# Two more tiles take their second product by seven products, and attention runs ahead of the tiles through DRAM

## The chip, the cores and the metric

The kernel runs on one core of one Trainium2 chip. Its time is the device time of one execution in microseconds (us); a comparison uses the median of the runs. The engines are named as in the profile: PE is TensorE's matrix multiplication and PEld its weight loads, DVE is VectorE, ACT is ScalarE, POOL is GpSimd, SP is SyncE, which here issues every DMA.

## The reference

The program is a linear attention with an RMS norm, followed by a feed-forward block with a SiLU gate. Everything is float32.

```python
q, k, v: (8 batches, 8 heads, 576 tokens, 64)     g_norm: (64,)
kv  = einsum('bhsd,bhse->bhde', k, v)             # 64 x 64 per batch and head
o   = einsum('bhsd,bhde->bhse', q, kv)
o   = o / sqrt(mean(o*o, -1) + 1e-6) * g_norm
x   = o.transpose(0, 2, 1, 3).reshape(4608, 512)  # tokens x features
h   = x @ w_in                                    # 512 -> 2048: the first product
out = (h * sigmoid(h)) @ w_out                    # 2048 -> 512: the second product
```

## The kernel before, in words

**Precision.** Every float32 operand of a product is held as two parts, an upper one rounded to the multiplier's format and a lower one, the rest. A product is three matmuls: upper by lower, lower by upper, upper by upper. The names ending in h and l (gh and gl, qh and ql) are such pairs.

**Tiles, blocks and steps.** The 4608 tokens are cut into nine tiles of 512, numbered 0 to 8. The hidden features are 16 blocks of 128, and the whole program is counted in blocks: block g = 16 t + n is place n of tile t, so tile 2 begins at block 32, tile 5 at block 80 and tile 7 at block 112. A batch of attention has 576 tokens, so it straddles two tiles.

**How a tile is multiplied.** Tiles 0 and 1 do both products plainly. From tile 2 on, the first product goes by seven products in place of eight (Strassen's scheme in Winograd's form, on halves of the weights and of x): two blocks are one step, and a step has 7 x 6 = 42 matmuls of 256 columns for it (`product`, L709), on sums of weight blocks that were formed once in tile 1, put into DRAM (`make_sums`) and loaded anew for each step (`load_sums`, L638). In `pair_step` (tiles 2 to 6) the second product is plain: 2 blocks x 4 banks x 3 terms x 2 halves = 48 matmuls per step (`project`, L494). In `seven_step` (tiles 7 and 8) the second product goes by seven products too: 42 matmuls per step (`multiply`, L880), with forms of the gated activations that DVE builds and sums of the second weights which `make_out_sums` has put into DRAM before and `load_out_sums` (L961) loads into small buffers for each step.

**Around a pair step.** PE does products 1, 2, 6 and 7; ACT copies product 1 (L761), DVE adds products 2, 6 and 7 to it (L762 to L764); PE does products 4, 5 and 3 into the same banks, and DVE adds those (L774 to L779). Then PE does the 48 matmuls of the step before. Product 5 writes the bank half that L762 has read.

**Around a seven step.** The products alternate in one bank with windows of the second product's matmuls. DVE reads the bank with L1075, L1093, L1107, L1108 and, behind product 3, L1116; the next step's product 1 waits for L1116. At the last three steps of tile 7, `spread_switch` and `made_ahead` form the operands of tile 8 in spare buffers, because tile 7's are in use to the end; `after_switch` empties the banks of tile 7 during the first steps of tile 8.

**Attention.** `plan(b, g)` books the work of batch b from block g on: k and v are loaded in blocks g-7 to g-4, their product (`kv_block`, L274) comes in block g-2, q is loaded from g-1 on, each of the four head pairs c is split in block g+c (L294, L295, L288), multiplied in g+2+c (`mm_out`, L307 to L309), squared and summed in g+3+c (L319, L320); the norms follow in blocks g+7 and g+8, and from g+9+c on `spread` (L327) lays out the norm and `scale` (L335) writes the scaled output. It writes straight to where a tile's x lies in full precision, two buffers called x32. A batch begins every 16 blocks, `plan(b, (b - 1) * NF)`, and its second part, which belongs to the next tile, is scaled in that tile.

**Order.** The order on each engine is the order in which the code is written (a manual schedule). Lists of jobs by block (`first_jobs`, `mid_jobs`, `last_jobs`) are run at the start, middle and end of a block. Each engine works its own queue in that order, SP's DMA issues too. Buffers turn in rings: the eight `kvq` buffers hold k, v, q and its parts (and in seven steps the gated activations and loaded sums), five `tmp` buffers hold passing work, four `opool` buffers hold attention's unscaled output o.

## Time and profile before

| | |
|---|---|
| median of 3 runs | 812.39 us (811.72 to 812.76) |
| the profiled execution | 813.5 us, span of its instructions 811.7 us |
| PE, PEld busy | 800.1 us (99%), 794.5 us (98%) |
| DVE, ACT, POOL busy | 585.2, 391.2, 194.5 us |
| granted TensorE clock | 0.998 |
| matmul records | 7388 |
| moved by DMA | 145.90 MB, 51.3% of the DMA engines' time in the kernel's own queue |

A row of groups reads: line, engine, operation, tile written <- tiles read (buffer numbers left out), shape, count | busy us, mean ns of one | idle time of the engine just before. A row of the timeline begins with the start from the span's beginning, and the time that it covers; [0.37 <-DVE gated L1116] is idle time before it and what ended it. A row of windows gives, for a stretch of time, the busy time and the count of PE, PEld, DVE, ACT and POOL, then the granted clock, the DMA engines' busy share and GB/s. The busy time of a matmul (277 ns) is longer than the distance from one to the next (113 ns), since they are pipelined: counts and starts tell the pace, busy time does not.

The tiles stand in the trace at these times: tile 2 from 203.2 us, and one more every 87.6 us up to tile 6 from 553.5 us; tile 7 from 641.1 us and tile 8 from about 724 us.

### The profile page before, as it was taken

To read this page: it belongs to the slowest core of one execution; us is meant where nothing else is said; L and a number is where in the kernel's file an instruction comes from. 1 tells how busy PE (TensorE), PEld (TensorE's weight loads), DVE (VectorE), ACT (ScalarE), POOL (GpSimd) and SP (SyncE) were. 2 spreads that over 40 slices of the span, in tenths; PEclk is the share of its full clock that TensorE was granted. 3 is DMA by queue.
4 is the path that set the end of the run, shared out by engine and by line. 5 is a ranking of instruction groups with operands and counts; after the bars stand their busy time and mean duration, and the time that the engine had idled before them with its cause. 6 is when DMAs were issued, how large, how long until landed. Compare 5 with 4: busy or idle time off the path is not lost.

```text
span 811.7 us, 18340 instructions
## 1 busy us (share of the span) xinstructions
PE 800.1 (99%) x7388; PEld 794.5 (98%) x7388; DVE 585.2 (72%) x1184; ACT 391.2 (48%) x825; POOL 194.5 (24%) x191
## 2 busy tenths in 40 slices
PE   8999999999999999999999999999999999999997
PEld 7899999999999999999999999999999999999996
DVE  4999956787566667757876667667875777788666
ACT  4887555434552255425642455336532543455443
POOL 2799783332110014020332014201402000000000
PEclk9999999999999999999999999999999999999999
DMA  9994012356434444465545462555443576667553
GB/s 350 412 409 127 1 60 78 131 182 248 167 101 162 163 155 140 142 218 190 170 152 179 154 236 91 204 185 193 147 140 104 187 253 212 214 209 223 198 185 115
DMA packets 60248, 145.90 MB, mean 180 GB/s; under 512 B 5891, under 2 KB 21251, under 8 KB 60163
## 3 DMA queue, kind: packets, MB, share of 16 engines
q1 hardware_dynamic: 60162, 144.73, 51.3%
q8 instruction: 58, 0.95, 0.5%
q14 instruction: 28, 0.22, 0.1%
HBM read 118.49 MB, written 26.21 MB: 178 GB/s over the span
## 4 chain that ended last, share of the span: by engine, by line
PE 91%; DMA 4%; POOL 2%; DVE 1%; issue 1%; ACT 0%; SPq 0%; DVEq 0%; POOLq 0%; ACTq 0%
PE acc L494 36%; PE hp L709 33%; PE hp L494 9%; PE acc L880 5%; DMA wi<-in_moe_w_in 3%; PE at L880 3%; PE at L274 2%; PE hp L880 1%; DMA k<-in_k 1%; PE at L307 1%; PE at L308 1%; PE at L309 1%; POOL wo L213 1%; DMA early_wo<-in_q 1%; POOL wi L213 0%
## 5 line engine op out<-in xcount | busy, mean ns | idle before, releaser
L494 PE MATMUL acc<-wo,gh 128*128 128x256 f32 x1792 | 279.6, 277 | 0.1
L494 PEld LDWEIGHTS acc<-wo,gh 128*128 128x128 f32 x1792 | 238.6, 188 | 0.6 <-POOL wo L213 0.3
L494 PE MATMUL acc<-wo,gl 128*128 128x256 f32 x896 | 174.5, 276 | 0.0
L709 PE MATMUL hp<-x_second,wi 128*128 128x256 f32 x1248 | 156.9, 277 | 0.0
L709 PEld LDWEIGHTS hp<-x_second,wi 128*128 128x128 f32 x1248 | 148.8, 188 | 0.0
L494 PEld LDWEIGHTS acc<-wo,gl 128*128 128x128 f32 x896 | 134.8, 188 | 0.0
L709 PE MATMUL hp<-operand,wi 128*128 128x256 f32 x1008 | 126.6, 277 | 0.4 <-DVE gated L1116 0.4
L709 PEld LDWEIGHTS hp<-operand,wi 128*128 128x128 f32 x1008 | 120.1, 188 | 0.6 <-DVE gated L1116 0.6
L295 POOL TENSOR_TENSOR ql<-q,qh 128x576 fp32r<-128x576 f32 x24 | 34.8, 1449 | 261.0 <-ACT qh L294 225.2
L761 ACT COPY wi<-hp 128x256 f32<-128x256 f32 x40 | 14.9, 372 | 92.6 <-PE hp L709 92.6
L719 ACT ACTIVATE gh<-gf 128x512 fp32r<-128x512 f32 x40 | 25.3, 633 | 57.1 <-DVE gf L774 52.5
L931 POOL TENSOR_TENSOR e<-e,partial 128x256 f32<-128x256 f32 x2 | 1.5, 730 | 190.3 <-DVE e L931 190.3
L494 PE MATMUL hp<-x_second,wi 128*128 128x256 f32 x384 | 46.3, 277 | 0.0
L826 ACT ACTIVATE gated<-gated 128x512 f32<-128x512 f32 x32 | 20.3, 633 | 52.8 <-DVE gated L1107 39.8
L494 PE MATMUL hp<-x,wi 128*128 128x256 f32 x360 | 44.5, 278 | 0.8 <-POOL x L445 0.8
L494 PEld LDWEIGHTS hp<-x_second,wi 128*128 128x128 f32 x384 | 44.9, 188 | 0.1
L603 POOL TENSOR_TENSOR s<-wo 128x512 f32<-128x512 f32 x16 | 21.6, 1353 | 93.3 <-DVE x L335 40.8
L494 PEld LDWEIGHTS hp<-x,wi 128*128 128x128 f32 x360 | 42.4, 188 | 1.1 <-POOL x L445 1.0
L719 ACT ACTIVATE gh<-wi 128x512 fp32r<-128x512 f32 x40 | 25.4, 635 | 36.8 <-DVE wi L774 32.8
L335 DVE SCALAR_TENSOR_TENSOR x<-o,gcol,yT 128x128 f32<-128x128 f32 (+7 forms) x52 | 41.2, 792 | 1.9
L762 DVE TENSOR_TENSOR wi<-hp,wi 128x256 f32<-128x256 f32 x20 | 8.5, 424 | 45.7 <-ACT wi L761 45.7
L313 ACT ACTIVATE sq<-at 128x256 f32<-128x256 f32 (+1 forms) x56 | 22.9, 409 | 37.8 <-PE at L309 37.5
(213 smaller groups left out, 1465.6 us busy)
## 6 DMA issues: line engine op xcount, KB each, us to landing
wi<-sums_in_dram SPq DMA_DIRECT2D x112, 512.0 KB, 3.3
s<-out_sums SPq DMA_DIRECT2D x48, 256.0 KB, 4.5
wi<-in_moe_w_in SPq DMA_DIRECT2D x16, 512.0 KB, 8.1
wo<-in_moe_w_out SPq DMA_DIRECT2D x16, 512.0 KB, 9.1
sums_in_dram<-sum_parts SPq DMA_DIRECT2D x16, 512.0 KB, 2.6
out_sums<-wi SPq DMA_DIRECT2D x16, 512.0 KB, 2.7
k<-in_k SPq DMA_DIRECT2D x28, 288.0 KB, 4.7
v<-in_v SPq DMA_DIRECT2D x28, 288.0 KB, 5.2
```

The lines of the kernel that those rows point to most:

```text
L274: nc.tensor.matmul(out=self.kv[h], lhsT=self.k[rows, c, :], rhs=self.v[rows, c, :], start=(start and r == 0), stop=(stop and r == 4),)
L295: (nc.vector if self.b == 1 else nc.gpsimd).tensor_tensor(out=self.ql, in0=self.q, in1=self.qh.bitcast(F32), op=ALU.subtract)
L313: nc.scalar.activation(out=self.sq[:, self.w], in_=self.ps, func=AF.Square)
L335: nc.vector.scalar_tensor_tensor(out=to, in0=self.o[:, a:e], scalar=gcol, in1=self.yT, op0=ALU.mult, op1=ALU.mult)
L494: nc.tensor.matmul(out=to[:, at:at + 256], lhsT=stationary, rhs=moving[:, at:at + 256], start=start and at == 0, stop=stop and at == n - 256,)
L603: nc.gpsimd.tensor_tensor(out=to, in0=w[:, 0, :], in1=w[:, 1, :], op=ALU.add)
L709: nc.tensor.matmul(out=out, lhsT=a_of(i, a, c), rhs=x[b][:, c], start=start and n == 0, stop=n == 5, skip_group_check=not check,)
L719: nc.scalar.activation(out=gh, in_=x, func=AF.Silu)
L761: nc.scalar.copy(out=p1, in_=u)
L762: nc.vector.tensor_tensor(out=c1[:, low], in0=v, in1=p1, op=ALU.add)
L826: nc.scalar.activation(out=self.gated, in_=self.gated, func=AF.Silu)
L880: nc.tensor.matmul(out=self.out[m], lhsT=g[m], rhs=self.weight(m, j, a), start=j == 0 and n == 0 and m in self.opens, stop=j == HF - 1 and ...
```

## The change

- `OUT7` goes from 7 to 5: tiles 5, 6, 7 and 8 run as seven steps, tiles 2 to 4 as pair steps.
- The batches of attention begin at blocks 16, 26, 36, 45, 55 and 64 (batches 2 to 7) in place of 16, 32, 48, 64, 80 and 96. Loads of k and v come one block later relative to that.
- From batch 3 on, `spread` and `scale` work on all 576 tokens of a head pair in one piece and write back to o in place. `keep`, one block later, stores o to a new DRAM tensor `x_in_dram` by tile, and `load_x` brings a tile's x back into the x32 buffers during the tile before (batch 2 does the same with its part that belongs to tile 3).
- The eight `make_out_sums` begin at blocks 34, 37, 40, 50, 53, 56, 66 and 69 in place of 52, 60, ... 108.
- `spread_switch` runs in tiles 5, 6 and 7. The spare buffers for the first two operands are taken once; later switches use the buffers that the switch before has freed.

```diff
-    OUT7 = 7
+    OUT7 = 5
+    AT = {1: 3, 2: 16, 3: 26, 4: 36, 5: 45, 6: 55, 7: 64}
...
+    x_in_dram = dram.tile([NT, 2, P, 2, TN], F32, name="x_in_dram")
+
+    def load_x(t):
+        for row in range(2):
+            nc.sync.dma_start(
+                out=late(row, [P, 2, TN], F32, f"x32_{row}").rearrange("p c n -> p (c n)"),
+                in_=x_in_dram[t, row].rearrange("p c n -> p (c n)"),
+            )
...
         def spread(self, y, segment):
-            a, e, _, _ = segments(self.b)[segment]
+            a, e = (0, S) if segment is None else segments(self.b)[segment][:2]
...
         def scale(self, segment):
-            a, e, t, o = segments(self.b)[segment]
-            to = self.o[:, a:e] if t < 2 else x32(self.c, slice(o, o + e - a))
+            a, e, t, o = (0, S, 3, 0) if segment is None else segments(self.b)[segment]
+            to = x32(self.c, slice(o, o + e - a)) if t == 2 else self.o[:, a:e]
...
+        def keep(self):
+            for a, e, t, o in segments(self.b):
+                if t > 2:
+                    nc.sync.dma_start(out=x_in_dram[t, self.c // 2][:, self.c % 2, o:o + e - a], in_=self.o[:, a:e])
...
     def spread_switch():
...
-        ahead.update({
-            1: spares, 6: [block6[:, 0], block6[:, 1]], 2: home(1), 7: home(6), 4: home(2), 5: home(7), 3: home(4),
-        })
+            once["spares"] = spare1, [block6[:, 0], block6[:, 1]]
+        ahead.update(zip((1, 6), once["spares"]))
+        ahead.update({2: home(1), 7: home(6), 4: home(2), 5: home(7), 3: home(4)})
+        once["spares"] = home(5), home(3)
...
-            for p, i in zip(ps, (-7, -6, -5, -4)):
-                at(first_jobs, g + i, lambda p=p: p.load(which="kv"))
+            for p, jobs, i in zip(ps, (last_jobs, first_jobs, first_jobs, first_jobs), (-6, -5, -4, -3)):
+                at(jobs, g + i, lambda p=p: p.load(which="kv"))
...
+        def x_stages(p, s, *parts):
+            for part in parts:
+                at(mid_jobs, s, lambda part=part: p.spread(norms[1][:, p.c], part), lambda part=part: p.scale(part))
+            if b > 1:
+                at(first_jobs, s + 1, p.keep)
...
-                x_stages(p, s + 2 + p.c, 0)
-            x_stages(p, b * NF + (1, 4, 6, 8)[p.c] if b >= OUT7 else b * NF + 1 + p.c, 1)
+                x_stages(p, s + 2 + p.c, *((0, 1) if b == 2 else (None,)))
...
-            plan(b, (b - 1) * NF)
+            plan(b, AT[b])
...
-        for j in range(HF):
-            spread_out(lambda j=j: make_out_sums(j), 3 * (3 * NF + 4 + 8 * j), 1, 1, 1, 1, 1, 1, 1, 1)
+        for t in range(3, NT):
+            at(last_jobs, max((t - 1) * NF + (5 if t - 1 > OUT7 else 2), AT.get(t, 0) + 14), lambda t=t: load_x(t))
+        for j, g in enumerate((34, 37, 40, 50, 53, 56, 66, 69)):
+            spread_out(lambda j=j: make_out_sums(j), 3 * g, 1, 1, 1, 1, 1, 1, 1, 1)
```

The lines of the changed file stand 10 to 18 places further down than those of the kernel before: L327 (spread) is L337 there, L335 (scale) L345, L701 (lower parts of the operands) L716, L723 (gl) L738, L762 to L764 are L777 to L779, L774 to L779 are L789 to L794, L839, L842, L847 are L854, L857, L862, and L1116 is L1134.

DVE in the first step of the first tile that runs as seven steps; before, this is tile 7 (block 112). The names are those of the forms (wi_8882) and of the half's gated activations; yT and o are attention's.

```order
L1107 TENSOR_TENSOR gated<-hp,wi_3139 128x256
L1108 TENSOR_TENSOR gated<-hp,wi_3139 128x256
L839 TENSOR_TENSOR wi_8882<-gated 128x256
L842 TENSOR_TENSOR wi_8882<-gated,wi_8882 128x128
L327 STREAM_TRANSPOSE yT<-y 128x512
L335 SCALAR_TENSOR_TENSOR x_0_1952<-o,gcol,yT 128x512
L1116 TENSOR_TENSOR gated<-hp,wi_3139 128x256
L847 TENSOR_TENSOR wi_8882<-gated,wi_8882 128x128
```

The same place in the changed kernel, tile 5 (block 80):

```order
L1125 TENSOR_TENSOR gated<-hp,wi_3269 128x256
L1126 TENSOR_TENSOR gated<-hp,wi_3269 128x256
L854 TENSOR_TENSOR wi_7035<-gated 128x256
L857 TENSOR_TENSOR wi_7035<-gated,wi_7035 128x128
L1134 TENSOR_TENSOR gated<-hp,wi_3269 128x256
L862 TENSOR_TENSOR wi_7035<-gated,wi_7035 128x128
```

Attention's spread and scale of the last batch no longer stand between the sums of the bank.

DVE in the last step of tile 2 (blocks 46 and 47), before:

```order
L723 TENSOR_TENSOR gl<-wi_3139,gh 128x512
L701 TENSOR_TENSOR operand_2948<-x_0_1952,operand_2948 128x512
L701 TENSOR_TENSOR operand_2952<-x_1_2124,operand_2952 128x512
L701 TENSOR_TENSOR operand_2987<-t_4031,operand_2987 128x512
L701 TENSOR_TENSOR x_second<-x_0_1952,x_second 128x512
L774 TENSOR_TENSOR wi_3139<-hp,wi_3139 128x512
L778 TENSOR_TENSOR gf<-hp,wi_3139 128x256
L779 TENSOR_TENSOR gf<-hp,gf 128x256
L701 TENSOR_TENSOR x_second<-t_4032,x_second 128x512
L701 TENSOR_TENSOR x_second<-t_4030,x_second 128x512
L701 TENSOR_TENSOR x_second<-x_1_2124,x_second 128x512
L723 TENSOR_TENSOR gl<-wi_3139,gh 128x512
```

and in the changed kernel, from the row of the fourth operand on (the rows ahead of it, gl and three operands, are as before):

```order
L716 TENSOR_TENSOR x_second<-x_0_1953,x_second 128x512
L337 STREAM_TRANSPOSE yT<-y 128x576
L345 SCALAR_TENSOR_TENSOR o<-o,gcol,yT 128x576
L789 TENSOR_TENSOR wi_3269<-hp,wi_3269 128x512
L793 TENSOR_TENSOR gf<-hp,wi_3269 128x256
L794 TENSOR_TENSOR gf<-hp,gf 128x256
L716 TENSOR_TENSOR x_second<-t_4337,x_second 128x512
L716 TENSOR_TENSOR x_second<-t_4335,x_second 128x512
L716 TENSOR_TENSOR x_second<-x_1_2125,x_second 128x512
L298 TENSOR_TENSOR kl<-kvm_91,kh 128x128
L738 TENSOR_TENSOR gl<-wi_3269,gh 128x512
L337 STREAM_TRANSPOSE yT<-y 128x576
```

A spread and a scale now stand ahead of L789 (before: L774), a second pair and two kl follow: attention's batch 4 is scaled and batch 5 split while the operands of tile 3 are made.

SP at the same turn in the changed kernel, last step of tile 2 and first of tile 3. The rows L653 load the sums of the first weights for the next step, L352 are the stores of `keep`:

```order
L352 DMA x_in_dram<-o 128x256
L352 DMA x_in_dram<-o 128x320
L273 DMA q<-in_q 128x576
L653 DMA wi_3083<-sums_in_dram 128x1024
L653 DMA wi_3085<-sums_in_dram 128x1024
L352 DMA x_in_dram<-o 128x256
L352 DMA x_in_dram<-o 128x320
L352 DMA x_in_dram<-o 128x256
L352 DMA x_in_dram<-o 128x320
L653 DMA wi_3083<-sums_in_dram 128x1024
```

Before, at this turn, nothing but loads of q and the stores of the tile's result stood between these loads at a turn of tiles. Now each pair of stores that waits for `scale` has loads of sums behind it.

More of the change, by code (lines that the diff above doesn't have):

```diff
@@ L985, in spread_switch @@
     def spread_switch():
[L987 to L994 removed]
+        if "spares" not in once:
+            once["partial"] = opool.tile([P, S], F32, name="partial", tag="o")[:, :TN].rearrange("p (j n) -> p j n", n=H)
+            spare1 = [
+                opool.tile([P, S], F32R, name="moved", tag="o")[:, :TN].rearrange("p (k n) -> p k n", k=2)
+                for _ in range(2)
+            ]
+            block6 = block("wi", HF + 7, F32R).rearrange("p a (k n) -> p a k n", k=2)
+            once["spares"] = spare1, [block6[:, 0], block6[:, 1]]
+        ahead.update(zip((1, 6), once["spares"]))
+        ahead.update({2: home(1), 7: home(6), 4: home(2), 5: home(7), 3: home(4)})
+        once["spares"] = home(5), home(3)
         x = sums_of_x()
@@ L1234, in linear_attention_rms_silu_ffn @@
         g_stats, stats = stats[:, 256:257], stats[:, :64].rearrange("p (c i j) -> p c i j", i=2, j=8)
-        second = plan(1, 3)
+        second = plan(1, AT[1])
         for item in ORDER.split():
```

10 lines of the change are left out of this document (1 added, 9 removed).

## The prediction

> **What bounds the kernel now.** I read the page's busy shares first, then the list of PE's waits, then the chain of waits through a pair step, and last the timeline of PE and DVE around the one wait that falls inside the tiles which change.
>
> ```profile
> PE 800.1 (99%) x7388; PEld 794.5 (98%) x7388; DVE 585.2 (72%) x1184; ACT 391.2 (48%) x825; POOL 194.5 (24%) x191
> PE 91%; DMA 4%; POOL 2%; DVE 1%; issue 1%; ACT 0%; SPq 0%; DVEq 0%; POOLq 0%; ACTq 0%
> PE hp L709 <- DVE gated L1116: 0.4, 1, 0.4
> ```
>
> PE is busy nearly to the end, 91% of the chain is PE, and the longest wait behind the start-up is 0.4 us, so the time is the number of matmuls times the distance from one to the next. That distance is read from the chain in tile 4:
>
> ```profile
> 360.76 4.76 PE hp L709 x42
> 365.52 5.44 PE acc L494 x48
> 370.96 4.76 PE hp L709 x42
> ```
>
> Starts follow each other without a hole: 42 matmuls of 256 columns in 4.76 us and 48 in 5.44 us are 113.3 ns each. A seven step has 84 of them, 9.52 us at this pace. But tile 7 does not keep it, and the windows of six steps of tile 7 and of five steps of tile 8 show this:
>
> ```profile
> 664.50:723.87 59.37, 59.37 (x507) 59.37 (x506) 46.28 (x107) 26.93 (x55) 0.00 (x0) 1.00 0.65 215
> 743.02:790.82 47.80, 47.80 (x422) 47.80 (x421) 31.04 (x79) 19.90 (x41) 0.00 (x0) 1.00 0.63 205
> ```
>
> 59.37 / 6 = 9.895 us a step in tile 7 (117.8 ns a matmul), 47.80 / 5 = 9.56 in tile 8. Granted clock (1.00 and 1.00) and DMA share (0.65 and 0.63) are alike, so neither is the reason. The timeline of PE shows where the slower pace begins and ends:
>
> ```profile
> 651.93 0.84 PE L709 MATMUL hp<-x_second,wi 128*128 128x256 f32 x6
> 654.51 1.68 PE L709 MATMUL hp<-operand,wi 128*128 128x256 f32 x12 [0.37 <-DVE gated L1116]
> 723.87 0.87 PE L709 MATMUL hp<-moved,wi 128*128 128x256 f32 x6
> 724.57 0.88 PE L709 MATMUL hp<-wi,wi 128*128 128x256 f32 x6
> 725.28 0.40 PE L880 MATMUL at<-wo,gh 128*128 128x256 f32 x2
> 743.02 0.84 PE L709 MATMUL hp<-moved,wi 128*128 128x256 f32 x6
> 743.70 0.87 PE L709 MATMUL hp<-wi,wi 128*128 128x256 f32 x6
> 744.41 0.40 PE L880 MATMUL at<-wo,gh 128*128 128x256 f32 x2
> ```
>
> Ahead of the wait six matmuls take 0.84 us (the last one's pipeline included), behind it six take 0.87: the pace turns from 113 to 118 ns at the 0.37 us wait and stays until 724.57, where product 6 of tile 8 reads its x from a weight block. From the first start behind the wait to the start of tile 8, 723.87 - 654.51 = 69.36 us pass for seven steps, against 7 x 9.52 = 66.6. The same thing happens once in the start-up, and there with other work:
>
> ```profile
> 24.85 0.52 PE L494 MATMUL acc<-x,wi 128*128 128x256 f32 x2 [0.24 <-POOL wi L213]
> 25.91 1.58 PE L494 MATMUL acc<-x,wi 128*128 128x256 f32 x12
> 27.32 0.87 PE L494 MATMUL hp<-x,wi 128*128 128x256 f32 x6
> 28.03 0.87 PE L494 MATMUL acc<-x,wi 128*128 128x256 f32 x6
> 28.74 0.38 PE L402 MATMUL at<-ident,on 128*128 128x128 f32 x2
> 55.22 0.41 PE L307 MATMUL at<-ql,kh 128*128 128x320 f32 x1 [0.74 <-ACT o L314]
> 55.77 2.90 PE L494 MATMUL hp<-x,wi 128*128 128x256 f32 x24
> 58.50 0.28 PE L307 MATMUL at<-ql,kh 128*128 128x256 f32 x1
> ```
>
> Behind the 0.24 us wait, 18 matmuls from 25.91 to 28.03 take 117.8 ns each, until matmuls of another shape come at 28.74. Behind the 0.74 us wait, 24 from 55.77 to 58.50 take 113.8: there other shapes (320 columns) follow at once. So a wait can put PE into a slower pace that lasts while only matmuls of one shape follow; how, the trace does not say.
>
> **The change, part by part.** *Fewer matmuls.* In tiles 5 and 6 the second product goes from 384 matmuls (8 steps x 48) to 8 x 42 = 336. That takes away 2 x 48 = 96 matmuls: 96 x 0.1133 = **-10.9 us**. Attention's matmuls move and keep their number.
>
> By the Trainium skill, TensorE: Matmul & The Clock Gate, Part 1, warm matmuls follow each other at N / 2.4 GHz + 2.5 ns, 109 ns at 256 columns, and the 96 would be worth 10.5 us by this estimate. The trace does not agree: 113.3 ns, so the row decides.
>
> *The opening wait.* In tile 7 the first seven step makes PE wait because L1116, which empties the bank, stands behind a spread and a scale of attention's last batch:
>
> ```profile
> 652.42 0.29 DVE L842 TENSOR_TENSOR wi<-gated,wi 128x128 f32<-128x128 f32 x1
> 652.63 0.70 DVE L327 STREAM_TRANSPOSE yT<-y 128x512 f32<-128x512 f32 x1
> 653.37 0.75 DVE L335 SCALAR_TENSOR_TENSOR x<-o,gcol,yT 128x512 f32<-128x512 f32 x1
> 654.03 0.42 DVE L1116 TENSOR_TENSOR gated<-hp,wi 128x256 f32<-128x256 f32 x1
> ```
>
> L1116 could start when product 3's last matmul is through (651.93 + 0.84 = 652.8), but starts at 654.03. In the changed kernel tile 5 opens the seven steps and no spread and scale stand there, since batch 7 is scaled in blocks 73 to 76. L1134 then ends about 653.3 on this clock, and PE wants it where its 0.37 us wait begins, 654.51 - 0.37 = 654.1. So it has 0.8 us to spare, the wait goes (-0.4), and with it, by the reading above, the slow pace of the seven steps that follow (66.6 - 69.4 = -2.7): **-3.1 us**. The other end is 0: another late sum in tile 5 starts the same pace there.
>
> *Spare operands.* Tiles 6 to 8 now read their operands from the buffers that a switch has moved them to. Tile 8 shows the price: 9.56 us a step against 9.52, with 0.71 us for the six matmuls of product 6 (744.41 - 743.70) against 0.68 for those of the product ahead (743.70 - 743.02). Two more tiles of eight steps: 16 x 0.04 = **+0.6 us**.
>
> *DVE and ACT in tiles 2 to 4.* Five batches that came every 16 blocks now come every 9 or 10. The work of a batch is the same, so its rows give its cost:
>
> ```profile
> L319 DVE STREAM_TRANSPOSE sqT<-sq 128x576 f32<-128x576 f32 x28 | 21.5, 769 | 0.0
> L288 DVE TENSOR_TENSOR kl<-kvm,kh 128x128 fp32r<-128x128 f32 x28 | 9.9, 354 | 1.0 <-ACT kh L287 0.8
> L335 DVE SCALAR_TENSOR_TENSOR o<-o,gcol,yT 128x448 f32<-128x448 f32 x4 | 3.8, 956 | 0.1
> L723 DVE TENSOR_TENSOR gl<-gf,gh 128x512 fp32r<-128x512 f32 x40 | 29.6, 741 | 1.8 <-ACT gf L720 1.8
> 372.76 0.42 DVE L762 TENSOR_TENSOR gf<-hp,wi 128x256 f32<-128x256 f32 x1 [1.63 <-ACT wi L761]
> 373.72 0.42 DVE L763 TENSOR_TENSOR wi<-hp,wi 128x256 f32<-128x256 f32 x1 [0.53 <-PE hp L709]
> 375.12 1.29 DVE L701 TENSOR_TENSOR operand<-x,operand 128x512 fp32r<-128x512 f32 x2
> 376.32 0.68 DVE L701 TENSOR_TENSOR operand<-t,operand 128x512 fp32r<-128x512 f32 x1
> 385.81 0.42 DVE L762 TENSOR_TENSOR wi<-hp,wi 128x256 f32<-128x256 f32 x1 [3.63 <-ACT wi L761]
> ```
>
> A spread of 576 costs the 0.77 us of L319 (same operation and shape), a scale in place 0.956 x 576 / 448 = 1.23. The fullest step is the last of tile 2 (blocks 46 and 47), where the built order has operands, two spreads with scales and two kl together: three sums at 0.42, three later ones (L774 counted like an operand of the same shape, 0.68, the two smaller at 0.42), two gl at 0.74, seven operands at 0.68, two kl at 0.35, two spreads with scales at 2.0: 13.8 us. Operations that follow each other at once start closer than their durations (two L701 in 376.32 - 375.12 = 1.20, 0.08 less each), so 21 of them need 13.8 - 1.7 = 12.1 us. PE's step there is 90 matmuls, 10.2 us, and six of attention's, 0.7. DVE falls behind by 1.2 us. It has 1.63 us idle ahead of the next L762, and product 5, which overwrites what L762 reads, starts at 370.96 + 30 x 0.1133 = 374.36, 1.2 us after L762 ends (373.18). So the lower end is 0. The upper end is that a turn, which my sum puts as good as full, is late at three such places by 1 us: 3 us. I take **+0.5**, nearer the lower end, because only this one turn has spreads and operands in the same step. Without that cover the full 1.2 us excess would be PE's.
>
> *Queues.* SP issues 108 DMAs more: loads of the second weights' sums for two tiles, the stores of `keep`, and the loads of x.
>
> ```profile
> wi<-sums_in_dram SPq DMA_DIRECT2D x112, 512.0 KB, 3.3
> 378.66 0.37 SPq L638 DMA_DIRECT2D wi<-sums_in_dram  x1
> out<-ob SPq DMA_DIRECT2D x30, 256.0 KB, 2.6
> ```
>
> 108 x 0.37 = 40 us more on a queue that paces nothing by itself. In the order a load of sums stands 78 matmuls ahead of its first use, 78 x 0.1133 = 8.8 us; it lands in 3.3, so 5.5 us are spare. A pair of stores ahead of it costs two issues, 0.7 us, and lands like the stores of out in 2.6 us, on buffers that the order gives over 7 us. What could eat the 5.5 us is the wait of a store for `scale`: the loads of sums are queued behind it, and PE's first product waits for them. I count 0, its other end being the last rival.
>
> **Sum** against the profiled execution: 813.5 - 10.9 - 3.1 + 0.6 + 0.5 = 800.6. That execution stands 1.1 us above the median of 812.39, so the forecast is 800.6 - 1.1 = **799.5 us**.
>
> **The rivals.** *B: the slow pace stays.* A sum in tile 5 is late all the same, or the first tile of seven steps has the pace for a reason of its own. For it: only 0.8 us are spare at the opening, more DMA runs, and the mechanism behind the pace is not known. Against it: the first products of tile 7, on the same buffers, ran at 113 ns until the wait, and the start-up shows the pace behind a wait as well. Then the second term is 0: 799.5 + 3.1 = 802.6 us.
>
> The same section of the Trainium skill makes the spacing depend on columns and clock alone, with a slow clock only after about 3.4 us of idleness. The clock of 1.00 in tile 7 agrees with the second part, the 117.8 ns do not fit the first; by that rule a wait of 0.37 us changes nothing later, which speaks for B.
>
> *C: DVE is late in tiles 2 to 4.* If three turns stall by 1 us, and each stall brings the slow pace for two pair steps until attention's other shapes end it (2 x 90 x 0.0045 = 0.8), that is 3 x 1.8 = 5.4 in place of 0.5: 804.4 us. For it speaks 12.1 against 10.9 us in that step; against it the 3.63 us that DVE idles ahead of L762 in the step behind.
>
> *D: SP waits for scale.* Should `scale` run more than 5.5 us later than the place of its store in SP's queue, every us beyond is PE's, 24 times (six batches, four head pairs). At 6.5 us it is 24 us: 799.5 + 24 = 823.5, slower than before; it costs more than the change saves from about 6.05 us on (12.9 / 24 = 0.54 beyond). Against it: DVE would have to be half a step behind at every batch, and it idles in each step.
>
> *That the change doesn't do what it says* I rule out: the built order has 96 matmuls fewer.
>
> **How the numbers follow.** The forecast has 0.54, B 0.27, C 0.12, D 0.07. Range: 0.5 us for stalls may be 0, and the saving a little more (the median's own spread is 0.5 us either way), 798.0; upward it takes in B and C to 805.0, which leaves out D and some of C. This kernel's measurement tells about 0.2% (1.6 us) from no change. Faster: all but D and a C that takes nearly everything, 0.92; the same: a D at the 0.54 us beyond, 0.02; slower 0.06.
>
> **What would show it.** Matmul records fall by about 96. PE's list of waits has no L1134 in tile 5, and windows there give 9.52 us a step (9.9 would be B); tiles 6 to 8 give 9.56. C shows as waits of L709 products for DVE at the turn to tile 3 and later, with steps above 10.9 us; D as SP's waits for L345 and PE's for the loads of sums. Wrong would be the whole reading if the pace changed in tile 5 with no wait ahead of it.

## The result, and the profile after

| | before | changed |
|---|---|---|
| median | 812.92 us (12 runs, 811.72 to 814.93) | 818.41 us (12 runs, 815.11 to 822.06) |
| the profiled execution | 813.5 us, span 811.7 | 815.11 us, span 813.3 |
| ratio | | 1.006, 95% interval 1.0041 to 1.0079 |

The change makes the kernel slower by 0.6%, where I had forecast 799.5 us and a range of 798.0 to 805.0. Its runs also spread more. The profiled execution is the fastest of its twelve, so the profile shows less of the loss than the median has. Three of the kernels below have one execution of 1325 to 2815 us, which their medians leave out; for one of them (two pairs of short matmuls in the kernel before) it is the profiled one, so only its time is read.

The first two rows are the page's busy times and chain of the changed kernel, the next three are from its list of PE's waits.

```profile
PE 791.6 (97%) x7292; PEld 784.4 (96%) x7292; DVE 624.0 (77%) x1280; ACT 411.0 (51%) x883; POOL 199.3 (25%) x191
PE 84%; DMA 7%; DVE 5%; POOL 2%; issue 1%; ACT 1%; SPq 0%; DVEq 0%; ACTq 0%; POOLq 0%
```

```profile
PE hp L724 <- DVE wi L777: 7.1, 4, 3.6
PE hp L724 <- DMA wi<-sums_in_dram: 1.9, 2, 1.2
PE hp L724 <- DVE gf L777: 1.3, 1, 1.3
```

7388 matmul records have become 7292: the 96 are gone. But PE's share of the chain falls from 91% to 84%, and PE now waits for L777 (which empties the bank half that product 5 writes; L762 before) five times and for loads of the first weights' sums twice. The timeline of PE shows where:

```profile
225.28 2.38 PE L724 MATMUL hp<-x_second,wi 128*128 128x256 f32 x18 [1.26 <-DVE gf L777]
262.31 2.33 PE L724 MATMUL hp<-x_second,wi 128*128 128x256 f32 x18 [1.23 <-DVE wi L777]
312.64 3.73 PE L724 MATMUL hp<-x_second,wi 128*128 128x256 f32 x18 [3.56 <-DVE wi L777]
360.70 2.31 PE L724 MATMUL hp<-x_second,wi 128*128 128x256 f32 x18 [0.70 <-DVE wi L777]
454.74 2.33 PE L724 MATMUL hp<-x_second,wi 128*128 128x256 f32 x18 [1.65 <-DVE wi L777]
610.23 0.97 PE L724 MATMUL hp<-wi,wi 128*128 128x256 f32 x6 [1.16 <-DMA wi<-sums_in_dram]
687.68 0.95 PE L724 MATMUL hp<-x_second,wi 128*128 128x256 f32 x6 [0.70 <-DMA wi<-sums_in_dram]
```

These are the steps that begin at blocks 34, 40, 48, 56, 72 (tiles 2 to 4), and 104 and 120 (tiles 6 and 7). Block 48 opens tile 3: the longest wait stands at the turn. Behind it PE runs on half its clock. The first two of these windows show this, the third covers seven steps of tile 5:

```profile
312.28:315.69 3.41, 3.05 (x14) 3.05 (x15) 3.25 (x7) 0.00 (x0) 0.00 (x0) 0.50 0.63 194
312.64:315.40 2.76, 2.76 (x13) 2.76 (x14) 2.69 (x5) 0.00 (x0) 0.00 (x0) 0.50 0.65 194
503.14:569.99 66.85, 66.85 (x590) 66.73 (x589) 47.82 (x115) 32.41 (x66) 0.00 (x0) 1.00 0.75 251
```

The half clock lasts 3.41 us, from 312.28 us on. Behind the wait, 13 matmuls in 2.76 us are 212 ns each: 1.3 us lost. Tile 5 opened without a wait and ran at 66.85 / 7 = 9.55 us a step, where 9.52 was forecast.

For all kernels below I measured each step of two blocks from the first matmul of its product 1 to that of the next step, and took away what its matmuls take at the even pace of the profile before (113.3 ns for 256 columns, attention's likewise). What is left is the loss of the step, in us. A wait, the half clock and the slow pace of 117.8 ns a matmul all count in it, and the last three columns hold every step of their tiles:

| profile | 34 | 40 | 46 | 48 | 56 | 58 | 72 | tiles 2-4 | tile 5 | tiles 6-7 |
|---|---|---|---|---|---|---|---|---|---|---|
| before | 0.1 | 0.0 | 0.2 | 0.0 | 0.0 | 0.0 | 0.0 | 1.0 | 0.3 | 3.4 |
| changed | 1.8 | 1.6 | 0.4 | 5.4 | 1.0 | 0.5 | 1.9 | 14.6 | 0.2 | 3.1 |
| changed, second profile | 1.8 | 1.2 | 1.0 | 5.5 | 1.8 | 0.5 | 1.7 | 16.5 | 0.0 | 2.0 |
| attention alone | 4.2 | 1.0 | 0.4 | 5.7 | 0.6 | 0.5 | 2.0 | 16.6 | 0.0 | 0.0 |
| ql on DVE | 3.4 | 2.1 | 0.4 | 1.9 | 1.2 | 0.1 | 1.9 | 14.6 | 0.3 | 1.9 |
| without DRAM | 4.9 | 1.0 | 0.1 | 6.1 | 0.7 | 0.5 | 1.9 | 18.2 | 2.4 | 0.8 |
| even places | 1.8 | 0.1 | 1.8 | 5.5 | 0.2 | 0.8 | 0.0 | 11.9 | 3.0 | 2.0 |
| + norms later | 0.2 | 0.1 | 3.7 | 5.7 | 0.5 | 0.9 | 0.0 | 16.2 | 3.0 | 2.7 |
| + ql of batch 5, late loads | 0.2 | 0.1 | 4.8 | 0.1 | 0.0 | 1.0 | 0.0 | 8.6 | 0.4 | 1.0 |
| + batch 5 behind the turn | 0.2 | 0.1 | 5.2 | 0.4 | 0.0 | 6.6 | 0.0 | 19.3 | 0.9 | 0.7 |
| mended | 0.2 | 0.1 | 0.3 | 1.3 | 1.0 | 0.1 | 0.0 | 6.3 | 3.0 | 0.9 |
| mended, turn as it was | 0.2 | 0.1 | 1.6 | 1.1 | 0.4 | 0.1 | 0.0 | 7.0 | 3.0 | 0.7 |

The balance of the two first profiles: 10.9 us fewer for 96 matmuls, 13.5 us more in tiles 2 to 4 (14.6 against 1.0), and 0.4 us fewer in tiles 5 to 7 together (3.3 against 3.7, where I had 2.5 fewer). That is 2.2 us up; between the two profiled executions it is 1.6, and the rest lies ahead of tile 2.

### The profile page after: what moved, and what is told of

It is laid out like the page before. It is cut to its first block, busy times and chain, and to the rows that moved or that the text cites. A ratio compares the mean times of both kernels' runs of the same rounds, so it can differ in the third digit from the quotient of the medians.

```text
span 813.3 us, 18521 instructions
## 1 busy us (share of the span) xinstructions
PE 791.6 (97%) x7292; PEld 784.4 (96%) x7292; DVE 624.0 (77%) x1280; ACT 411.0 (51%) x883; POOL 199.3 (25%) x191
## 4 chain that ended last, share of the span: by engine, by line
PE 84%; DMA 7%; DVE 5%; POOL 2%; issue 1%; ACT 1%; SPq 0%; DVEq 0%; ACTq 0%; POOLq 0%
PE hp L724 31%; PE acc L509 23%; PE acc L895 10%; PE hp L509 9%; PE at L895 5%; DMA wo<-in_moe_w_out 3%; PE hp L895 3%; PE at L284 2%; DMA wi<-sums_in_dram 2%; DMA early_wo<-in_q 1%; PE at L317 1%; PE at L318 1%; PE at L319 1%; DMA out_sums<-wi 1%; POOL wo L223 1%
## 5 line engine op out<-in xcount | busy, mean ns | idle before, releaser
L509 PE MATMUL acc<-wo,gh 128*128 128x256 f32 x1280 | 200.9, 277 | 0.3 <-POOL wo L223 0.3
L509 PEld LDWEIGHTS acc<-wo,gh 128*128 128x128 f32 x1280 | 171.2, 188 | 0.7 <-POOL wo L223 0.5
L509 PE MATMUL acc<-wo,gl 128*128 128x256 f32 x640 | 124.9, 276 | 0.0
L724 PEld LDWEIGHTS hp<-operand,wi 128*128 128x128 f32 x912 | 109.6, 188 | 0.1
L509 PEld LDWEIGHTS acc<-wo,gl 128*128 128x128 f32 x640 | 96.5, 188 | 0.0
L841 ACT ACTIVATE gated<-gated 128x512 f32<-128x512 f32 x64 | 40.5, 633 | 97.9 <-DVE gated L1125 75.3
L895 PE MATMUL acc<-wo,gh 128*128 128x256 f32 x256 | 46.8, 276 | 0.0
L895 PE MATMUL acc<-s,gs 128*128 128x256 f32 x288 | 42.9, 276 | 0.0
L895 PEld LDWEIGHTS acc<-wo,gh 128*128 128x128 f32 x256 | 38.5, 188 | 0.0
L895 PEld LDWEIGHTS acc<-s,gs 128*128 128x128 f32 x288 | 37.3, 188 | 0.0
L1110 ACT COPY gated<-hp 128x256 f32<-128x256 f32 x32 | 11.9, 373 | 49.4 <-PE hp L724 49.4
L854 DVE TENSOR_TENSOR wi<-gated 128x256 f32<-128x256 f32 x64 | 27.2, 425 | 10.9 <-ACT gated L841 9.8
```

Of the source, the lines that this page charges most:

```text
L509: nc.tensor.matmul(out=to[:, at:at + 256], lhsT=stationary, rhs=moving[:, at:at + 256], start=start and at == 0, stop=stop and at == n - 256,)
L724: nc.tensor.matmul(out=out, lhsT=a_of(i, a, c), rhs=x[b][:, c], start=start and n == 0, stop=n == 5, skip_group_check=not check,)
L841: nc.scalar.activation(out=self.gated, in_=self.gated, func=AF.Silu)
L854: nc.vector.tensor_tensor(out=f[:, 0:2], in0=y[:, 1:3], in1=y[:, 0:1].to_broadcast([P, 2, P]), op=ALU.subtract)
L895: nc.tensor.matmul(out=self.out[m], lhsT=g[m], rhs=self.weight(m, j, a), start=j == 0 and n == 0 and m in self.opens, stop=j == HF - 1 and ...
L1110: nc.scalar.copy(out=first.gated[:, low], in_=u)
```

## The experiments

**Attention alone.** Does the loss come with attention's new places, or with the two tiles of seven products?

```diff
-    OUT7 = 5
+    OUT7 = 7
```

> The changed kernel with OUT7 = 7: attention runs ahead through DRAM as in the change, but tiles 5 and 6 keep the plain second product. Theory D (DVE): the time is lost in tiles 2 to 4, where attention's DVE work now meets the tile's, so the steps there lose the same 13 to 14 us against their matmuls as in the changed kernel, tiles 5 and 6 run at 10.2 us a step, and tile 7 opens without a wait: 812.9 - 3.1 + 13.5 = 823 us, slower than both kernels. Theory M (DMA): the loads of the second weights' sums for two more tiles and the stores and loads of x crowd the queue; with the former gone most of the loss goes as well: 812.9 - 3.1 + 5 = 815 us or less.

Measured: 825.38 us, ratio 1.0163 (1.0148 to 1.0178). Tiles 2 to 4 lose 16.6 us, at the same steps; two rows of PE's timeline there:

```profile
226.79 3.22 PE L724 MATMUL hp<-x_second,wi 128*128 128x256 f32 x18 [2.20 <-DVE gf L777]
315.33 3.10 PE L724 MATMUL hp<-x_second,wi 128*128 128x256 f32 x18 [3.56 <-DVE wi L777]
```

So the loss of tiles 2 to 4 comes without the two more tiles, and the loads for these are not needed to explain it. What it comes with is attention's new places or those of the second weights' sums, which this run keeps as well: three of the losses turn out below to be the sums'. The waits for sums in tiles 6 and 7 are gone here. Step 34 loses 4.2 us with a wait of 2.20: behind it the clock falls to a half, as a window of this run shows.

```profile
228.50:230.00 1.50, 1.50 (x10) 1.27 (x9) 1.43 (x3) 0.00 (x0) 1.29 (x2) 0.50 0.05 11
```

The Trainium skill, TensorE: Matmul & The Clock Gate, Part 1, halves the clock after an idle stretch of about 3.4 us. The 3.56 us at block 48 agree; this half clock behind 2.20 us does not. The wait at the same place in the next run, 2.90 us, brought none (1.00 in its window), and neither did one of 3.42 us in the run "Norms later", as PE's timeline and a window of that run show:

```profile
298.03 2.33 PE L724 MATMUL hp<-x_second,wi 128*128 128x256 f32 x18 [3.42 <-DVE gf L777]
298.03:304.00 5.97, 5.97 (x52) 5.97 (x53) 5.90 (x9) 2.75 (x6) 1.87 (x1) 1.00 0.60 220
```

So the length of a wait alone does not tell whether the clock falls.

**ql on DVE.** In steps 46 and 48 of the changed kernel single DVE operations are far too long. The rows are of the timeline of DVE and of POOL; L777, the last of DVE's, is the one for which PE waits 3.56 us:

```profile
298.73 2.53 DVE L716 TENSOR_TENSOR operand<-x,operand 128x512 fp32r<-128x512 f32 x2
307.38 1.92 DVE L738 TENSOR_TENSOR gl<-wi,gh 128x512 fp32r<-128x512 f32 x1
309.23 0.77 DVE L337 STREAM_TRANSPOSE yT<-y 128x576 f32<-128x576 f32 x1
310.03 0.82 DVE L345 SCALAR_TENSOR_TENSOR o<-o,gcol,yT 128x576 f32<-128x576 f32 x1
310.76 1.49 DVE L298 TENSOR_TENSOR kl<-kvm,kh 128x128 fp32r<-128x128 f32 x1
312.18 0.41 DVE L777 TENSOR_TENSOR wi<-hp,wi 128x256 f32<-128x256 f32 x1
299.07 1.64 POOL L305 TENSOR_TENSOR ql<-q,qh 128x576 fp32r<-128x576 f32 x1 [5.15 <-ACT qh L304]
307.24 1.52 POOL L305 TENSOR_TENSOR ql<-q,qh 128x576 fp32r<-128x576 f32 x1 [6.53 <-DMA x_in_dram<-o]
310.61 1.49 POOL L305 TENSOR_TENSOR ql<-q,qh 128x576 fp32r<-128x576 f32 x1 [1.85 <-ACT qh L304]
```

A kl usually takes 0.28 us, here 1.49, as long as the ql of POOL that began just ahead of it; two L716 took 1.29 before, a gl 0.68. Three such holds add 3.7 us to DVE at this turn, and from 305.38 us to L777 it has no idle time. The Trainium skill, SBUF — State Buffer, section "SBUF: two separate sides", says that a DVE operation with two inputs in SBUF and a GpSimd operation that reads SBUF exclude each other, and whichever starts first keeps the other out for its whole length. The trace agrees.

```diff
-            (nc.vector if self.b == 1 else nc.gpsimd).tensor_tensor(   # ql
+            nc.vector.tensor_tensor(
```

> The changed kernel with the lower part of q (ql, L305) formed on DVE in place of POOL. In the profile single DVE operations are 1 to 1.3 us longer than usual where a ql of POOL runs (kl 1.49 in place of 0.28 us, gl 1.92 in place of 0.68). If DVE's lateness in tiles 2 to 4 comes from being held by POOL there, the holds go, DVE pays 0.7 for each ql, and the excess of the turn of tile 3 falls by 2 us or more: 812 to 816 us. If it is plain lack of time on DVE, 20 more operations of 0.7 us make it worse: 819 to 824 us.

Measured: 815.04 us, ratio 1.0033 (1.0013 to 1.0054). Step 48 falls from 5.4 to 1.9 us, but steps 34 and 40 and others rise by as much: tiles 2 to 4 lose 14.6 us, as before. So the holds make most of the turn's loss. That the others rise because DVE now does the ql itself fits, but is not shown; neither theory alone is right.

**Without DRAM.** Is it the stores of o and the loads of x? Left out are both, so tiles 3 to 8 multiply a stale x.

```diff
-                at(first_jobs, s + 1, p.keep)
...
-            at(last_jobs, max(...), lambda t=t: load_x(t))
```

> The changed kernel without the stores of o to DRAM and the loads of x from it (tiles 3 to 8 then multiply a stale x; all else is as it was). Theory M: the waits of PE for loads of sums in tiles 6 and 7 (1.2 and 0.7 us) go, and so does most of the 3.6 us wait at the turn of tile 3 with its 2.8 us of half clock, because ACT and POOL wait there behind stores of o: 818.4 - 7 = 811 us, and runs spread less than the 815 to 822 of the changed kernel. Theory D: only the two waits go, 816 us.

Measured: 816.03 us, ratio 1.0042 (1.0019 to 1.0065), runs from 812.96 to 821.11. Tiles 2 to 4 lose 18.2 us, the turn 6.1. The stores of o are not the cause there, nor of the spread, and my theory M falls; 816 us is what D had. The waits for sums in tiles 6 and 7 are gone: these do come from the loads of x, since the last stores of o are issued in tile 4. In the changed kernel's chain and SP timeline they look so:

```profile
603.32 6.87 DMA wi<-sums_in_dram
```

```profile
599.52 0.80 SPq L153 DMA_DIRECT2D x<-x_in_dram  x2
603.32 4.53 SPq L653 DMA_DIRECT2D wi<-sums_in_dram  x2
```

A load of sums, which lands in 3.8 us by the median of this kernel, took 6.87 us behind 1 MB of x and three loads of the second weights' sums (0.75 MB).

**Tile 7 of the kernel before opened without a wait.** This tests the term of -3.1 us where it was read.

```diff
-            x_stages(p, b * NF + (1, 4, 6, 8)[p.c] if b >= OUT7 else b * NF + 1 + p.c, 1)
+            x_stages(p, b * NF + (0, 4, 6, 8)[p.c] if b >= OUT7 else b * NF + 1 + p.c, 1)
```

> The kernel before, with the spread and scale of batch 7's first head pair one block earlier (block 112 in place of 113), so that they no longer stand ahead of L1116 in tile 7's opening step. If the slow pace of 117.8 ns is set off by the 0.37 us wait there, tile 7 runs at 9.52 us a step and the time is 812.9 - 3.1 = 809.8 us. If the pace belongs to the first tile of seven steps, the steps stay at 9.9 us: 812.5 us.

Measured: 812.16 us, ratio 0.9993 (0.9983 to 1.0003). The wait is gone from PE's list and the first two steps run at 10.20 and 9.52 us (10.73 and 10.00 before). But in the third step, with no wait in the list near, the slow pace comes all the same. PE's timeline there (such a group takes 1.52 us at the even pace), and a window of tile 7:

```profile
668.31 1.65 PE L709 MATMUL hp<-x_second,wi 128*128 128x256 f32 x12
669.00:719.00 50.00, 50.00 (x427) 50.00 (x426) 38.43 (x88) 22.95 (x46) 0.00 (x0) 1.00 0.66 218
```

427 matmuls in 50 us, as in tile 7 before (507 in 59.37). So the pace did not hang on this wait. But the trace has something there that the list of waits leaves out: the first of the twelve matmuls at 668.31 is followed after 194 ns in place of 113, and the pace begins behind it.

**Even places for the sums of the second weights.** Steps 40, 56 and 72 follow the three sums begun at odd blocks (37, 53, 69). What stands there, from ACT's and DVE's timelines of the changed kernel:

```profile
258.38 0.62 ACT L624 CAST wi<-s 128x512 fp32r<-128x512 f32 x1 [2.22 <-DMA out_sums<-wi]
260.73 0.31 ACT L297 CAST kh<-kvm 128x128 fp32r<-128x128 f32 x1
259.04 0.69 DVE L625 TENSOR_TENSOR wi<-s,wi 128x512 fp32r<-128x512 f32 x1 [3.25 <-ACT wi L624]
261.12 0.81 DVE L298 TENSOR_TENSOR kl<-kvm,kh 128x128 fp32r<-128x128 f32 x1
261.85 0.41 DVE L777 TENSOR_TENSOR wi<-hp,wi 128x256 f32<-128x256 f32 x1
```

The two halves of a sum share one buffer. ACT's L624 for the second half stands 2.22 us for the store of the first (2.8 us in the median); DVE's L625 stands 3.25 us for ACT; then come sqT, sums and kl, and L777 last. DVE was not out of time here: it stood idle.

```diff
-        for j, g in enumerate((34, 37, 40, 50, 53, 56, 66, 69)):
+        for j, g in enumerate((34, 38, 42, 50, 54, 58, 66, 70)):
```

> The changed kernel with the second weights' sums begun at blocks 34, 38, 42, 50, 54, 58, 66, 70, all even, in place of 34, 37, 40, 50, 53, 56, 66, 69. In the profiles the steps 40, 56 and 72 lose 1.6, 1.0 and 1.9 us; they are the ones that follow the three odd places, and there ACT's L624 stands 2 us and more for the store of the sums' first half (DMA out_sums<-wi), with kh, and behind it kl and L777, queued after it. Theory Q (a place in the queue): these three losses go, steps 34 and 48 stay as they are, and the time falls by 4 us: 814 us. Theory D (DVE has too little time in tiles 2 to 4): the losses move to other steps and the time stays at 817 to 819 us.

Measured: 815.78 us, ratio 1.0063 (1.0046 to 1.008). Steps 40, 56 and 72 lose 0.1, 0.2 and 0.0 us, as Q has it. But step 46 now loses 1.8, and tile 5 of this profile loses 3.0 us, by a wait of 0.85 us for a load and the slow pace behind it, so the time of the profiled execution does not show it. The median lies between the figures of the two theories.

**Norms later.** Step 34: two copies of a result and nine operations of the norms stand ahead of L777 on DVE (rows of its timeline in the changed kernel).

```profile
221.48 1.28 DVE L548 COPY ob<-acc 128x512 f32<-128x512 f32 x2
222.79 0.80 DVE L477 COPY m<-sums 32x72 f32<-32x72 f32 x4
224.66 0.23 DVE L258 SCALAR_TENSOR_TENSOR y<-u,y 128x72 f32<-128x72 f32 x1
224.81 0.42 DVE L777 TENSOR_TENSOR gf<-hp,wi 128x256 f32<-128x256 f32 x1
```

```diff
-            spread_out(lambda: rsqrt(*norms, False), 3 * s + 2, 6, 3, 3, 3)
+            spread_out(lambda: rsqrt(*norms, False), 3 * s + 4, 6, 6, 3)
```

> As the run before, and the norms of batches 2 to 7 (15 small DVE operations each) begin two thirds of a block later, in portions of 6, 6 and 3 in place of 6, 3, 3 and 3, so that for batch 3 none of them stands ahead of L777 in step 34. By Q step 34 loses nothing any more (1.8 to 4.9 us in the runs so far): 811.5 us. By D the norms only move into the same step's second half and L789 is late instead: 814 us.

Measured: 814.36 us, ratio 1.0039 (1.0018 to 1.006). Step 34 falls to 0.2, as Q has it. But the same edit puts nine operations of batch 4's norms into the stretch ahead of step 46's L777, and step 46 rises to 3.7: the loss moved, as D has it, though to another step than D names.

**ql of batch 5 on DVE, loads of x later.**

```diff
-            (nc.vector if self.b == 1 else nc.gpsimd).tensor_tensor(   # ql
+            (nc.vector if self.b in (1, 5) else nc.gpsimd).tensor_tensor(
...
-            at(last_jobs, max((t - 1) * NF + (5 if t - 1 > OUT7 else 2), AT.get(t, 0) + 14), lambda t=t: load_x(t))
+            for row in range(2):
+                at(last_jobs, max((t - 1) * NF + (6 if t - 1 > OUT7 else 2), AT.get(t, 0) + 14)
+                   + 3 * row * (t - 1 > OUT7), lambda t=t, row=row: load_x(t, row))
```

> As the run before, and two more edits: for batch 5 alone, whose split stands at the turn to tile 3, DVE forms ql in place of POOL; and the two loads of x for tiles 7 and 8 come one and four blocks later, one by one. If POOL's hold on DVE makes the loss of 5.4 us in step 48, it falls to 2 us or less as in the run with every ql on DVE, without that run's losses elsewhere; if loads of x make PE wait for the sums in steps 104 and 120 (1.5 and 1.0 us), these losses go. Both: 806 us. Neither: 811 us.

Measured: 810.67 us, ratio 0.999 (0.9974 to 1.0005): level with the kernel before. Step 48 loses 0.1 in place of 5.7; steps 104 and 120 lose next to nothing, and tiles 6 and 7 fall to 1.0 in all. Step 46 loses 4.8: a wait of 2.94 us, and half the clock behind it. That is about as much as the time lies above the 806 us expected.

**Batch 5 behind the turn.**

```diff
-    AT = {1: 3, 2: 16, 3: 26, 4: 36, 5: 45, 6: 55, 7: 64}
+    AT = {1: 3, 2: 16, 3: 26, 4: 36, 5: 48, 6: 57, 7: 66}
```

> As the run before, but ql stays on POOL throughout, and batches 5, 6 and 7 begin at blocks 48, 57 and 66 in place of 45, 55 and 64, so that batch 5's split no longer meets the operands of tile 3 and batch 4's scaling. By D as a matter of place the loss of step 48 goes altogether, and nothing new comes as long as batch 6 and 7 keep clear of the turn to tile 4 (blocks 62 and 63): 804 to 806 us. If the turn is too full without batch 5 as well, 2 us of it stay: 808 us.

Measured: 816.47 us, ratio 1.006 (1.004 to 1.0079). Step 48 loses 0.4, with ql on POOL: without batch 5's split at the turn its loss is gone, as expected. But step 46 loses 5.2 without batch 5, and step 58 now 6.6, where batch 5's norms, scaling and batch 6's split meet the sums begun at 58. So the expected time was wrong: the split was not what filled the turn alone, and its new place brought a new loss.

**Mended.** The places above are mended together, some of them otherwise than in the runs above (ql of batches 3, 4 and 7 in place of 5, the norms of three batches only, some sums at other blocks, batch 7 one block later), with three more edits at the turn: batch 4's first two scalings ahead of it, tile 3's sums of x four thirds of a block earlier, and a third of a block more between the two halves of a sum.

```diff
+    AT = {..., 7: 65}
+            (nc.vector if self.b in (1, 3, 4, 7) else nc.gpsimd).tensor_tensor(   # ql
+            spread_out(lambda: rsqrt(*norms, False), *((3 * s + 4, 6, 6, 3) if b in (2, 3, 7) else (3 * s + 2, 6, 3, 3, 3)))
+                x_stages(p, s + 2 + {4: (0, 0, 2, 3)}.get(b, (0, 1, 2, 3))[p.c], ...)
+            spread_out(sums_of_x, 3 * (t * NF - 3) + {3: -4}.get(t, 0), 1, 1, 1, 1)
+        for j, g in enumerate((34, 38, 41, 50, 53, 58, 67, 71)):
+            spread_out(lambda j=j: make_out_sums(j), 3 * g, 1, 1, 1, 1, 1, 1, 1, 0, 1)
```

> The changed kernel's mathematics and loads with the places of the work mended by what the runs so far showed: the second weights' sums begin at blocks 34, 38, 41, 50, 53, 58, 67, 71 with a third of a block more between the sums' two halves (so that ACT does not stand for the store of the first), the norms of batches 2, 3 and 7 begin two thirds of a block later, ql of batches 3, 4 and 7 on DVE, batch 4's first two spreads and scales ahead of the turn to tile 3, tile 3's sums of x four thirds of a block earlier, batch 7 one block later, and the two loads of x for tiles 7 and 8 later and one by one. If the loss of tiles 2 to 4 is the order on DVE's and ACT's queues (theory Q), all of it but 1 to 3 us goes, the slow pace of PE may or may not come (0 to 3 us), and the time is 799 to 804 us, 1% to 1.5% below the kernel before. If DVE has too little time there (theory D), the loss moves on and the time stays at 808 us or above.

> As the run before, with tile 3's sums of x (four DVE operations of 0.7 us) back at their old place, blocks 45 and 46, in the last step but one and the last of tile 2. The turn to tile 3 is then the one place where DVE has more to do than the step is long, and steps 46 and 48 together lose 2 to 5 us more than in the run before, all else alike: 802 to 808 us. If the turn is relieved enough by batch 4's earlier scaling, both runs are the same.

> The changed kernel once more, for a second profile and times beside the mended one. The losses of steps 34, 40, 48, 56 and 72 stand again at 1 to 6 us each, since they are an order's; the steps at 117.8 ns a matmul, which come and go without a wait in the profiles so far, lie elsewhere than in the first profile, and so account for a part of the spread of 815 to 822 us.

Measured side by side: mended 806.03 us, ratio 0.9919 (0.99 to 0.9937); with the sums of x back at the turn 807.73, 0.9947 (0.9928 to 0.9965); changed again 817.77, 1.0087 (1.006 to 1.0113). 806.03 lies between the ranges of Q (799 to 804) and D (808 or above). PE's longest waits behind the start-up in the mended kernel, and its busy times:

```profile
PE hp L723 <- DVE wi L776: 2.2, 3, 1.0
PE 792.8 (98%) x7292; PEld 786.3 (98%) x7292; DVE 626.6 (78%) x1292; ACT 411.0 (51%) x883; POOL 180.8 (22%) x179
```

DVE does as much as in the changed kernel (626.6 and 624.0 us), and tiles 2 to 4 lose 6.3 us in place of 14.6 to 16.5; 1.1 us of the 6.3 are the slow pace in steps 74 to 78. So most of the loss was the order and POOL's holds, not the amount of DVE's work. This run does not part the two. The runs above do for single steps: the even places took 4.2 us from steps 40, 56 and 72, and ql of batch 5 on DVE took 5.6 from step 48. The sums of x back at the turn add 1.1 us to steps 46 and 48, less than the 2 to 5 that I expected; the intervals of the two runs overlap. The second profile of the changed kernel has the same five losses at the same steps. The slow pace lies partly elsewhere in it, and it holds about 730 matmuls from tile 2 on, in place of 320 (3.2 and 1.4 us). The slow pace fills tile 5 of the mended kernel (seven steps of it, windows):

```profile
496.16:565.41 69.25, 69.25 (x590) 69.25 (x589) 48.13 (x115) 32.38 (x66) 0.00 (x0) 1.00 0.72 243
```

The same 588 matmuls took 66.85 us in the changed kernel's profile.

**Short matmuls against the slow pace.** One matmul of 256 columns is made as two of 128: in each step of seven products, first in the kernel before, then in the mended one; then in two steps of the first such tile only.

```diff
-                nc.tensor.matmul(out=out, lhsT=a_of(i, a, c), rhs=x[b][:, c], ...)
+                for w in (slice(0, P), slice(P, H)) if cut and n == 1 else (slice(0, H),):
+                    nc.tensor.matmul(out=out[:, w], lhsT=a_of(i, a, c), rhs=x[b][:, c, w], ...)
...
-        product(1, i, u, True, False)
+        product(1, i, u, True, False, True)      # then: t == OUT7 and i in (1, 4), mended: (0, 4)
```

> The kernel before, with one matmul of 256 columns per step of tiles 7 and 8 (the second of product 1) made as two of 128: the same sums, no other change. In all profiles the stretches at 117.8 ns end where matmuls of another shape come (kv's of 64 columns, the norm's of 128) or at a turn of tiles, and they begin with a wait in some and without one in others. If a pair of short matmuls ends the slow pace, tile 7 has at most part of its steps at 9.9 us, and the time is 812.5 - 2.5 + 16 x 0.03 = 810 to 811 us. If the pace has nothing to do with the shapes, tile 7 stays at 9.9 us a step and the time is 812.5 + 0.5 = 813 us.

> The mended kernel with the same edit in its tiles 5 to 8. Its profile has 3.0 us of slow pace in tile 5. If short matmuls end it, 803 to 804 us; if not, 806 to 807 us.

Measured: 813.5 us, ratio 1.0015 (1.0005 to 1.0025), and 807.39, 0.9936 (0.9923 to 0.9949). In the first, PE's timeline in tile 7 shows the place of the pair with which the slow pace ends (x13: a product of 12 with one matmul cut in two), and ahead of it the pair at the wait with which the pace begins:

```profile
656.73 1.79 PE L710 MATMUL hp<-operand,wi 128*128 128x256 f32 x13 [0.37 <-DVE gated L1117]
665.19 0.87 PE L710 MATMUL hp<-x_second,wi 128*128 128x256 f32 x6
666.84 1.65 PE L710 MATMUL hp<-operand,wi 128*128 128x256 f32 x13
```

The six ahead of the second pair still take 0.87 us. The windows of 8 us ahead of it and behind it:

```profile
657.00:665.00 8.00, 8.00 (x70) 8.00 (x70) 4.63 (x11) 4.87 (x11) 0.00 (x0) 1.00 0.98 323
668.32:676.00 7.68, 7.68 (x70) 7.68 (x69) 5.40 (x12) 2.41 (x5) 0.00 (x0) 1.00 0.66 217
```

The same 70 matmuls take 8.00 and 7.68 us. The DMA share differs too, but tile 7 of the kernel before kept the slow pace at 0.65. Tile 7's last steps run at 9.65 us in place of 9.89. But a pair costs 0.13 us itself: tile 8 goes from 9.56 to 9.69 a step. So the pair at 666.84 ended the pace, the one right behind the wait at 656.73 did not keep it from beginning, and 16 pairs cost at least as much as they save. In the mended kernel with pairs the pace stood in tile 4 alone and ended ahead of the first pair, so that run does not test it.

> The kernel before with the pair of short matmuls only in steps 1 and 4 of tile 7 (2 cuts at the 0.13 us that each cost in the run with 16 of them). If short matmuls end the slow pace and nothing else starts it again, six of tile 7's steps run at 9.52 in place of 9.89 us: 812.6 - 6 x 0.37 + 0.3 = 810.6 us. If the lower steps of the run with 16 pairs came only from having a pair in every step, tile 7 falls back to 9.9 us between the pairs, and the time is 812.9 us.

> The mended kernel with the pair in steps 0 and 4 of tile 5 only: 806.0 - 2.8 + 0.3 = 803.5 us if short matmuls end the slow pace for good, 806.3 us if not.

Measured: 813.03 us, ratio 1.0007 (0.9995 to 1.002), and 804.81, 0.9908 (0.9891 to 0.9924). In the mended kernel's profile tile 5 began at the even pace, the slow one began behind a wait of 0.47 us for a load in step 3, and ended at the pair of step 4. The gain over the mended kernel (0.9908 and 0.9919) is within the intervals; on the kernel before there is none.

## Why the prediction was wrong

- **Fewer matmuls, -10.9 us: right.** 7388 - 7292 = 96, and but for three steps with an interruption (86, 104, 120) the steps of tiles 5 to 8 are as long as worked out.
- **Spare operands, +0.6 us: right.** 9.56 us a step in tiles 6 to 8.
- **The opening wait, -3.1 us: right in this profile, 2.7 of it by luck.** L1134 did not make PE wait, and tile 5 ran at 9.55 us a step. But taking away the wait in the kernel before left the slow pace, and tile 5 of the other kernels has it in some profiles (2.4 to 3.0 us) and not in others. In the run without DRAM it begins in tile 5 with no wait in the list ahead of it, which the prediction named as the sign that its reading is wrong. Rival B's doubt was the right one. Only the 0.4 us of the wait itself can be counted on.
- **DVE and ACT in tiles 2 to 4, +0.5 with ends of 0 and 3: the step that failed.** It measured 13.5 us. I summed DVE's work of one step against PE's length, and three things were not in the sum. First, the place in the queue: ACT standing for a store (steps 40, 56, 72) and norms ahead of L777 (34) cost 1 to 2 us each. Where ACT stood for the store, DVE was idle for 3.25, 1.01 and 2.79 us (steps 40, 56 and 72): DVE had time there, and the order wasted it. The kernel before has the same single buffer, but all its sums begin at even blocks. Second, POOL's holds, 1.2 us each and 3.7 us in all at the turn, which loses 5.4; the mean of kl in my fence, 354 ns where it usually takes 0.28 us, already held some of them, and it is 520 now. Third, half the clock behind the longest wait, 1.3 us and more. The scale, on the other hand, I had put too high: 0.82 us at the turn where my sum has 1.23. "Only this one turn" was wrong too: five steps lose.
- **Queues, 0: too low by 2 us.** Not the stores of o but the loads of x crowd the loads of sums, in tiles 6 and 7.
- **Rival C came nearest.** PE does wait for DVE in tiles 2 to 4. But C put three stalls of 1.8 us at the turns, 804.4 us in all, with the slow pace behind each; in fact there are five of 1.0 to 5.4 us, only one of them at a turn, and at three DVE itself waited for ACT. Nor do attention's other shapes always end the pace: in the profile of "Norms later" it goes on behind matmuls of 320 columns.
- **Rival D did not happen.** SP does wait for `scale`, but no load of sums in tiles 2 to 4 makes PE wait:

```profile
SPq L352 <- DVE o L345: 43.7, 16, 6.0
```

What stays open: the median lies 3.3 us above the profiled run, and no profile of so slow an execution of the changed kernel was taken; and what starts the slow pace. The two may belong together. The profile of "Norms later" is of an execution of 820.24 us, where that kernel's others took 811.54 to 816.39, and about 1580 matmuls stand at the slow pace in it, 7 us in all. That the pace makes the spread is likely by this, but not shown.

## What to carry to other kernels

When a change packs more work beside a bound engine, do not sum a step's work against its length: go through each helper engine's queue and ask, for the one operation that frees the bound engine's buffer, what stands ahead of it and what that waits for. A single buffer between two halves, a store and a compute, is a wait that was hidden only as long as the neighbours were far away. And places are cheap to move: nearly the same work in better places, twelve ql moved from POOL to DVE, turned 0.6% slower into 0.8% faster than the kernel before.

## What the runs showed of the hardware

- PE runs matmuls of 256 columns at 113.3 or at 117.8 ns each, at a granted clock of 1.00 in both. In the profiles above nearly every stretch of the slower pace from tile 2 on begins where one matmul follows another late, be it by a wait (0.37 us in tile 7 before) or by less than the list of waits shows (194 ns in place of 113 with the opening free, 126 in tile 5 without DRAM). About as many such places start nothing: a wait of 1.65 us at block 72 of the changed kernel did not. The pace lasts through hundreds of matmuls and ended at a pair of 128 columns, at attention's matmuls of 64, at some waits, and at the turn to tile 6 or 8. What it is was not found.
- A DVE operation with two inputs in SBUF can take the length of a POOL operation on top of its own: kl 1.49 in place of 0.28 us.
- Half the granted clock for 3.41 us (312.28 to 315.69 in the changed kernel) came with waits of 3.56, 2.94 and 2.20 us, but not with waits of 3.42 and 2.90 us, nor with any of 1.65 and less.
